# Wide tap products for half of the channels, loads from a second queue, and small re-cuts in a fused S4 convolution and MLP kernel

## The chip, the cores and the metric

The kernel runs on one core of one Trainium2 chip. The metric is the device time of one execution in microseconds (us); the median of several executions is compared. Five engines work side by side, each on its own list of instructions in a fixed order, and wait for each other by semaphores: PE (TensorE, matrix products into PSUM), DVE (VectorE), ACT (ScalarE), POOL (GpSimd), and SP (SyncE), which here only issues DMAs. A core has 16 DMA engines, shared by all queues.

## The reference, cut to what matters

Sequence length L = 2048, width D = 512, N = 128 modes for each channel, MLP width F = 1376, batch 1, all inputs bf16.

```python
# S4 mixer
dt = exp(log_dt)[:, None];  A = A_re + 1j*A_im
P = exp((dt*A)[:, :, None] * arange(L))               # 512 x 128 x 2048, complex
K = einsum("dn,dnl,dn->dl", C, P, dt*B).real          # one filter of 2048 taps for each channel
y = irfft(rfft(pad(u)) * rfft(pad(K)))[:L] + u*Dskip  # causal convolution by FFT of length 4096
# block
h  = x + S4(layernorm(x))
h2 = h + (gelu(layernorm(h) @ w1 + b1) @ w2 + b2)
```

The cost is in K: for each channel 2048 taps out of 128 complex modes, and in the two convolution transforms, which the kernel does as products.

## The kernel before, in words

**Taps.** A tap index l is the sum of a coarse and a fine part. For each channel d the kernel holds two small tables over the 128 modes (the modes lie on the partitions): EB/IB with NB = 33 coarse entries (real and imaginary part) and EA/IA with NA = 20 fine entries. The taps of a channel are then one product of 20 x 128 by 128 x 33, real and imaginary part summed in PSUM. The 512 channels are four chunks of 128 (CW); `kgen(c)` (from L1009) does one chunk. Its products have 20-column weights and 33 moving columns, and four channels stand at four column positions of the array, 32 rows apart: 256 products for a chunk (L1024 the real part, L1025 the imaginary one). The results are copied from PSUM to the tile `Kg` in two copies of 726 and 330 elements a partition.

**The tables.** Magnitudes come from exponentials on ACT: `bexps` (L738, 32 exponentials) for B and `aexps` (L948 to L953) for A, where PE adds up the exponents in PSUM with weights WA, a scaled identity for each step between entries; these scaled identities are made on ACT (L695) or DVE (L697) early. Phases come from `chain` (L959): PE adds integer phases step by step (L976 to L985), ACT takes the sine (L991), and DVE multiplies the table by sine and cosine (L1000 to L1002). There are four chains in this order: chunks 0 and 1, B and A, and chunks 2 and 3, B and A. GpSimd prepares the weights of the chains, among them the field words (L641 on).

**Convolution.** The signal (x after layer norm, `unorm`, L884) is transformed in `austage` (L897), written to DRAM (AU_d, one for each half of the sequence), read back in another layout (X0, XB; `xspec` L904), and finished by products (`fstage`, L923). The taps take the same way: `kspec` (L1061), the DRAM tensors AK_d, and `fstage`. `inverse` (L1085) multiplies the two spectra on DVE (L1101), transforms on PE (L1111), and a transposing DMA (`turn`, L1117) brings the result to ZT0 and ZT1, one tile for each chunk.

**Tails and MLP.** The rows are worked off in two halves b of two sub-blocks sb, each of four tiles j of 128 rows. `tail(b, sb)` (L1172) adds the residual x by a product with the identity (L1184), the convolution by products with DD (L1189), copies the sum from PSUM to `hs` and takes its statistics (L1194), normalises (L1208, L1210) and transposes. `mlp(b, sb)` (L1227) does 44 products (L1239), 11 gelus (L1241) and 44 products (L1256) of 512 columns, and adds h on DVE (L1258), which also frees PSUM, into one of three output tiles `ots`, from which two DMAs write 64 rows each.

**What sets the order.** Nothing of this is issued where it stands in the code. `S.add(engines, cost, function, reads, writes)` gathers all operations with planned costs and a priority `S.pr`. `S.run(NSL)` then lists them by a simulation of its own with four PSUM slots of 128 x 1024 f32 (`Ps()` takes one); `RANK`, a table of a place for each (priority, engine), breaks ties. `evac` (L530) lets the plan choose ACT (L533) or DVE (L535) for a copy out of PSUM. The instructions are emitted in the planned order, and each engine keeps it on the chip. Nearly all DMAs stand in the order of SP's list (`dma`, L543; L545).

The waits of the list that matter: a slot's next use waits for the copies out of it; `hs`, w1 and w2, and XB lie in memory that the tables held, so their loads wait for the products on these tables.

Of the kernel before, what the change touches and what calls it, by code (L numbers as in the profile page):

```python
# [145 lines left out]

class VS(V):
# [15 lines left out]
    "0S": 55, "0A": 268, "0.01A": 132, "0.02S": 110, "0.03A": 277, "0.04S": 66, "0.05S": 164, "0.1S": 223, "0.1A": 283, "0P": 86, "0.05P": 38,  # L163
    "0.1D": 241, "0.7D": 13, "0.75P": 173, "0.6P": 275, "0.72P": 230, "0.3D": 46, "0.1P": 244, "0.2P": 146, "0.05A": 95, "0.06A": 157, "0.07A": 106,
    "0.08A": 239, "0.09A": 193, "0.5D": 297, "0.5P": 290, "0.2A": 73, "0.2D": 2, "1.01A": 43, "1.015A": 131, "1.02A": 145, "1.025A": 229, "1.03A": 143,
    "1.035A": 342, "1.04A": 285, "1.045A": 121, "1.05A": 195, "1.055A": 316, "1.06A": 228, "1.065A": 181, "1.07A": 57, "1.075A": 11, "1.08A": 163,
    "1.085A": 84, "1.09A": 180, "1.095A": 25, "1.1A": 93, "1.105A": 155, "1.11A": 220, "1.115A": 29, "1.12A": 274, "1.125A": 255, "1.13A": 261,
    "1.135A": 133, "1.14A": 31, "1.145A": 170, "1.15A": 122, "1.155A": 337, "1.16A": 348, "1.165A": 62, "0.4A": 22, "0.4P": 254, "0.401A": 306,
    "0.4D": 12, "0.41D": 5, "0.42D": 71, "0.6A": 167, "0.6D": 212, "0.5S": 343, "0.55D": 78, "0.55S": 339, "1.5D": 90, "1.3P": 221, "1.55D": 309,
    "1.4P": 209, "1.5P": 51, "1.2D": 75, "1.201D": 79, "1.202D": 67, "1.203D": 35, "8D": 72, "8S": 213, "0.95P": 208, "0.95A": 17, "1.05P": 328,  # L170
    "1.15P": 253, "1.25P": 60, "1.25A": 191, "1.35P": 4, "1.35A": 105, "1.45P": 111, "1.45A": 246, "1.55P": 289, "1.55A": 325, "1.65P": 178,
    "1.65A": 299, "1.75P": 34, "1.75A": 242, "1.85P": 63, "1.85A": 45, "8A": 7, "1.3A": 102, "1.3D": 295, "1.7P": 219, "1.71P": 0, "1.9A": 58,
    "2.05P": 202, "1.8P": 42, "1.81P": 113, "2.11P": 26, "2P": 184, "2A": 324, "2D": 161, "2.1P": 112, "2.1A": 226, "2.1D": 207, "2.2P": 314,
    "2.2A": 280, "2.2D": 169, "2.3P": 340, "2.3A": 205, "2.3D": 83, "2.5P": 80, "2.5A": 187, "2.5D": 264, "2.6P": 320, "2.6A": 256, "2.6D": 152,
    "2.7P": 130, "2.7A": 298, "2.7D": 189, "2.8P": 96, "2.8A": 134, "2.8D": 101, "2.9P": 270, "2.9A": 1, "2.9D": 50, "2.94A": 27, "3.2D": 88,
    "4.1D": 117, "2.98A": 352, "2.96A": 326, "2.963A": 338, "2.966A": 162, "2.95A": 336, "4.5P": 350, "1.72P": 159, "3.4D": 284, "3.401D": 293,
    "3.402D": 115, "3.403D": 190, "3.5P": 149, "3.5A": 85, "3.5S": 251, "3.501P": 247, "3.501A": 312, "3.501S": 243, "4P": 302, "4A": 303, "4D": 234,
    "4.1P": 235, "4.1A": 345, "4.2P": 287, "4.2A": 135, "4.2D": 192, "4.3P": 39, "4.3A": 291, "4.3D": 174, "4.5A": 233, "4.5D": 301, "4.6P": 3,
    "4.6A": 91, "4.6D": 19, "4.7P": 292, "4.7A": 236, "4.7D": 154, "4.8P": 273, "4.8A": 259, "4.8D": 142, "4.9P": 310, "4.9A": 18, "4.9D": 151,
    "4.1S": 37, "4.101P": 271, "4.101A": 238, "4.101S": 116, "4.2S": 281, "4.201P": 222, "4.201A": 171, "4.202P": 41, "4.202A": 214, "4.203P": 6,  # L180
    "4.203A": 69, "5.1P": 36, "5.1A": 118, "5.11P": 108, "5.11A": 262, "5.11D": 89, "9.1P": 294, "9.1A": 266, "9.11P": 232, "9.11A": 198, "9.11D": 48,
    "9.2P": 147, "9.2A": 346, "9.21P": 218, "9.21A": 260, "10.2P": 224, "10.2A": 330, "10.21P": 124, "10.21A": 176, "10.2S": 20, "10.25S": 201,
    "10.25P": 166, "10.25A": 127, "10.251P": 240, "10.251A": 32, "10.252P": 99, "10.252A": 129, "10.253P": 168, "10.253A": 267, "10.3D": 64,
    "10.3P": 341, "10.3A": 329, "10.3S": 40, "10.4D": 47, "10.4P": 44, "10.4A": 182, "10.4S": 33, "13.1P": 318, "13.1A": 203, "13.11P": 179,
    "13.11A": 351, "13.11D": 103, "17.1P": 331, "17.1A": 197, "17.11P": 327, "17.11A": 120, "17.11D": 70, "17.2P": 165, "17.2A": 56, "17.21P": 237,
    "17.21A": 24, "17.2S": 49, "17.25S": 126, "17.25P": 141, "17.25A": 288, "17.251P": 104, "17.251A": 353, "18.2P": 278, "18.2A": 252, "18.21P": 300,
# [17 lines left out]
class Clock:  # L204
# [12 lines left out]
    def work(self, t, c, a):  # L217
        self.idle(t)
        while c > 1e-9:
            k = 1.0 if self.warm else 2.0  # L220
            d = min(c * k, self.end - t)
            t += d
            c -= d / k
            self.act += a * d / k
            if self.end - t < 1e-9:
                self.turn()
        return t


class Sched:  # L230
    def __init__(self):
        self.ops = []
        self.wr, self.rd = {}, {}
        self.pr = 0.0
# [174 lines left out]
def kernel(ctx, tc, A_u, A_A_re, A_A_im, A_B_re, A_B_im, A_C_re, A_C_im, A_log_dt, A_Dskip,  # L409
# [40 lines left out]
    def at(lo, dt, *shape):  # L450
        return V(ar, lo, dt, shape)
# [934 lines left out]
```

## Time and profile before

| what | us |
|---|---|
| median of 3 runs | 286.64 |
| the three runs | 286.47, 286.64, 288.91 |
| the profiled execution | 284.77 |
| its span | 283.0 |
| mean granted clock of PE | 0.957 |
| first exponential of `bexps` | 8.77 |
| end of the exponentials | 38.4 |
| first product of the first chain | 47.1 |
| end of the fourth chain | 102.2 |
| taps of chunks 2 and 3 | 103.8 to 126.4 |
| first product of the MLP | 189.1 |
| last output sum | 278.46 |

The span is what the profiler shows of the program; the execution's time has 1.8 us more around it. "Busy" of an engine counts its instructions' time without waits. An entry such as `L1101 DVE ar<-ar 128x1024 x48 | 30.0, 685` is a group: line, engine, operation, output and input, count, busy time in us and the mean of one in ns. Nearly all SBUF data lies in one large tile called `ar`. The chain of work that ended last follows back, from the last instruction, what released each step; "issue" in it is time in which an engine waited for nothing that the profile shows, "SPq" time in which SP's queue issued.

### The profile page before, as it was taken

How to read it: one execution, taken by the hardware profiler on the slowest of the kernel's cores; microseconds unless marked ns; L12 is line 12 of the kernel's file. 1: busy time of each engine (PE TensorE's matmuls, PEld its weight loads, DVE VectorE, ACT ScalarE, POOL GpSimd, SP SyncE). 2: the span in 40 equal slices, each digit the busy share in tenths (PEclk: the TensorE clock that was granted, in tenths of full speed). 3: DMA queues.
4: the chain of work that ended last, by engine and by line, in shares of the span. 5: the costliest groups of instructions: out<-in, count | busy, mean ns of one | idle time of the engine just before them, and what ended most of it. 6: DMA issues, size and time to landing. Idle time of an engine off the chain costs nothing.

```text
span 283.0 us, 7899 instructions
## 1 busy us (share of the span) xinstructions
PE 227.0 (80%) x3316; PEld 122.8 (43%) x3316; DVE 177.2 (63%) x380; ACT 176.5 (62%) x241; POOL 40.9 (14%) x213
## 2 busy tenths in 40 slices
PE   6407949679999897299978767879999989979973
PEld 2202413324577756243666653544343434434431
DVE  4999899999989770039979973876378320021020
ACT  5999999999959884046876733378326704603600
POOL 9991001006980000000000000000000000000000
PEclk9999986999999999869999995799999999999999
DMA  7950013879300008995279999951215310011011
GB/s 148 316 113 0 1 46 94 219 222 302 90 3 5 5 5 287 345 384 157 80 193 232 242 197 223 184 116 38 57 41 102 74 37 22 19 37 37 1 39 37
DMA packets 47878, 33.62 MB, mean 119 GB/s; under 512 B 29441, under 2 KB 43746, under 8 KB 47842
## 3 DMA queue, kind: packets, MB, share of 16 engines
q1 hardware_dynamic: 46642, 32.72, 45.6%
q8 instruction: 26, 0.43, 0.6%
q10 hardware_dynamic: 1200, 0.39, 0.6%
q14 instruction: 10, 0.08, 0.1%
HBM read 16.32 MB, written 10.49 MB: 95 GB/s over the span
## 4 chain that ended last, share of the span: by engine, by line
PE 46%; ACT 17%; DVE 15%; DMA 11%; issue 7%; SPq 2%; POOL 1%; DVEq 0%; ACTq 0%; POOLq 0%
PE ps L1239 14%; PE ps L1256 13%; DMA ar<-ar 6%; ACT ar L738 6%; ACT ar L533 4%; DVE ar L535 4%; PE ps L1024 3%; DMA ar<-AK_d 3%; PE ps L1025 3%; PE ps L923 3%; PE ps L1189 3%; DVE ar L1101 2%; ACT ar L991 2%; PE ps L985 2%; DVE ar L1258 2%
## 5 line engine op out<-in xcount | busy, mean ns | idle before, releaser
L533 ACT CAST ar<-ps 128x1024 bf16<-128x1024 f32 (+3 forms) x77 | 66.4, 907 | 54.6 <-PE ps L1025 15.2
L1241 ACT ACTIVATE ar<-ps,ar 128x512 bf16<-128x512 f32 (+1 forms) x44 | 29.9, 686 | 30.1 <-PE ps L1239 29.3
L1256 PE MATMUL ps<-ar 128*128 128x512 bf16 (+1 forms) x176 | 40.3, 379 | 5.0 <-DVE ar L1258 5.0
L1258 DVE TENSOR_TENSOR ar<-ps,ar 128x512 bf16<-128x512 f32 x16 | 11.0, 689 | 48.8 <-PE ps L1256 43.5
L535 DVE CAST ar<-ps 128x1024 bf16<-128x1024 f32 (+2 forms) x27 | 31.0, 1169 | 16.2 <-PE ps L923 13.0
L1239 PE MATMUL ps<-ar 128*128 128x512 bf16 (+1 forms) x176 | 39.1, 379 | 0.0
L991 ACT ACTIVATE ar<-ps 128x1024 bf16<-128x1024 int16 x36 | 35.2, 1066 | 2.3 <-issue 1.1
L1101 DVE TENSOR_TENSOR ar<-ar 128x1024 bf16<-128x1024 bf16 x48 | 30.0, 685 | 4.6 <-PE ps L1111 4.2
L1111 PE MATMUL ps<-ar 64*128 64x128 bf16 x768 | 26.9, 225 | 5.4 <-DVE ar L1101 4.5
L1256 PEld LDWEIGHTS <-ar 128*128 128x128 bf16 (+1 forms) x176 | 16.9, 98 | 27.4 <-issue 8.0
L1111 PEld LDWEIGHTS <-ar 64*128 64x128 bf16 x768 | 23.3, 99 | 10.1 <-DVE ar L1101 8.0
L581 POOL TENSOR_SCALAR ar<-ar 128x128 bf16<-128x128 bf16 (+5 forms) x40 | 24.8, 643 | 18.2 <-ACT ar L602 18.2
L1024 PE MATMUL ps<-ar 128*20 128x33 bf16 x512 | 19.9, 249 | 8.5 <-issue 7.9
L1239 PEld LDWEIGHTS <-ar 128*128 128x128 bf16 (+1 forms) x176 | 17.4, 100 | 20.6 <-issue 0.6
L985 PE MATMUL ps<-ar 128*32 128x256 f16 x560 | 21.4, 275 | 2.0 <-ACT ar L991 1.1
L1024 PEld LDWEIGHTS <-ar 128*20 128x20 bf16 x512 | 17.8, 124 | 10.7 <-issue 10.0
L923 PE MATMUL ps<-ar 128*64 128x512 bf16 (+1 forms) x160 | 19.2, 367 | 3.1 <-DMA ar<-AK_d 2.1
L1025 PE MATMUL ps<-ar 128*20 128x33 bf16 x512 | 19.9, 248 | 0.0
L1194 DVE BATCH_NORM_STATS2 ar<-ps 128x6 f32<-128x512 f32 x16 | 10.7, 691 | 13.5 <-ACT ar L533 7.9
L1001 DVE TENSOR_TENSOR ar<-ar 128x1024 bf16<-128x1024 bf16 x26 | 18.0, 711 | 1.7 <-ACT ar L991 1.6
L985 PEld LDWEIGHTS <-ar 128*32 128x32 f16 x560 | 13.8, 97 | 10.8 <-issue 9.8
L1002 DVE TENSOR_TENSOR ar<-ar 128x1024 bf16<-128x1024 bf16 x26 | 17.4, 697 | 1.6 <-ACT ar L991 1.5
(86 smaller groups left out, 265.0 us busy)
## 6 DMA issues: line engine op xcount, KB each, us to landing
AU_d<-ar SPq DMA_DIRECT2D x16, 256.0 KB, 4.6
ar<-AU_d SPq DMA_DIRECT2D x8, 512.0 KB, 5.2
ar<-AK_d SPq DMA_DIRECT2D x8, 512.0 KB, 7.8
ar<-in_A_u_dram SPq DMA_DIRECT2D x16, 128.0 KB, 3.8
ar<-in_A_u_dram SPq DMA_DIRECT2D x4, 512.0 KB, 5.7
AK_d<-ar SPq DMA_DIRECT2D x2, 1024.0 KB, 4.7
AK_d<-ar SPq DMA_DIRECT2D x4, 512.0 KB, 3.8
out_dram<-ar SPq DMA_DIRECT2D x32, 64.0 KB, 2.0
```

The lines of the kernel that those rows point to most:

```text
L533: act.copy(out_fn(), in_fn())
L535: dve.tensor_copy(out_fn(), in_fn())
L923: pe.matmul(pst(p)[64 * h:64 * h + 64, w * (k + r):w * (k + r) + w], lhsT=T.ap()[:, f, r, :], rhs=v.ap()[:, f, :], start=True, stop=True, ...
L985: pe.matmul(pst(p)[32 * g:32 * g + 32, 256 * j:256 * j + 256], lhsT=W2[DELTAS.index(d)].ap(), rhs=S2[g].ap()[:, ch0:ch0 + 256], start=Fals ...
L991: add("ACT", c_act(1024), lambda e, p=p, sc=sc, cs=cs: act.activation(sc[cs].ap().rearrange("p a b -> p (a b)"), pst(p, i16).rearrange("p ...
L1024: pe.matmul(o, lhsT=Ar.ap()[:, :, d], rhs=Br.ap()[:, :, d], start=True, stop=False, tile_position=(0, 32 * g))
L1025: pe.matmul(o, lhsT=Ai.ap()[:, :, d], rhs=Bi.ap()[:, :, d], start=False, stop=True, tile_position=(0, 32 * g))
L1101: dve.tensor_tensor(o, a, b_[:, :, ::-1, :] if sw else b_, ALU.mult)
L1111: pe.matmul(pst(p)[:, 512 * h + 128 * k:512 * h + 128 * k + 128], lhsT=q.ap()[rows, 2 * k + r, :], rhs=TP[w].ap()[rows, f0 // 2 + k, :], s ...
L1239: pe.matmul(pst(p)[:fs, 512 * z:512 * z + 512], lhsT=w1s[dc].ap()[:, fc * P:fc * P + fs], rhs=ybuf.ap().rearrange("p (t c) k -> p c t k", ...
L1241: add("ACT", c_act(512, 1), lambda e, p=p, z=z, fc=fc, fs=fs: act.activation(hT.ap()[:fs, fc, :], pst(p)[:fs, 512 * z:512 * z + 512], ACT. ...
L1256: pe.matmul(pst(p)[:, 512 * z:512 * z + 512], lhsT=hT.ap()[:fs, fc, 128 * t:128 * t + 128], rhs=w2s[fc].ap()[:fs], start=(fc == 0), stop=( ...
```

## The change

- *Taps of chunks 2 and 3.* `kgen4` replaces `kgen` there. EA2 and IA2 hold these chunks' A tables channel by channel, 20 entries padded to 32, so that four channels are 128 weights. One product takes them with 132 moving columns (four channels of 33). Of the 4 x 4 blocks of the result only the four on the diagonal are wanted: each is copied by itself, 32 partitions of up to 198 elements. The pads are cleared by GpSimd. 64 products a chunk replace 256, and 24 copies replace 2.
- *Tables.* `aexps` goes by halves of 256 channels, four entries an exponential; the second half writes the new layout. WA has 20 scaled identities (steps of 12 entries instead of 6), made by GpSimd. The last chain's sines and products on DVE work in the new layout (runs of 4 elements). Raw inputs are transposed by products with a permuted identity, which puts the channels in an order that suits the new taps.
- *Loads.* x, w1, w2, b2 and the second half's signal spectrum (XB) are issued by GpSimd's queue, in fewer and larger DMAs; SP keeps the inputs of the start, AU_d of the first half, AK_d, the transposes and the output. The plan knows both queues, and a transpose waits in the plan for what is in transfer.
- *Layer norm.* The inverse square root takes two iterations with other constants, not three: four small operations fewer.
- *Tails.* All but the first take the residual on DVE, which adds `hs` to PSUM and takes the statistics from SBUF; the product with the identity and the copy go.
- *Output.* Eight tiles `ots` instead of three.
- *Plan.* All entries of `RANK` are new, so the order moves everywhere. On SP the reads of AK_d for chunks 2 and 3 now stand after three of the four writes. In the last product of each MLP sub-block the four tiles' products alternate otherwise.

```diff
+    def pad(v, k):
+        POOL(3.3, lambda: gp.memset(v.ap().rearrange("p c d a -> p (c d) a")[:, :, NA:32], 0.0), w=[v], pr=k)
...
-    LD = [LA[a] - (LA[a - 6] if a >= 6 else 0) for a in range(NA)]
+    LD = [LA[a] - (LA[a - 12] if a >= 12 else 0) for a in range(NA)]
...
+        PTS(WA[n], identb, float(v), pr=0.8 + 0.01 * (n // 4))
...
-        for _ in range(3):
+        for m, k in ((-1.0, c1), (-0.5 * c0 ** 3, 1.5 * c0)):
...
+    def kgen4(c, pr):
+        Ar, Br, Ai, Bi = EA2[c - 2], EB[c], IA2[c - 2], IB[c]
+        kg = Kg[c // 2]
+        for j0 in range(0, 32, 6):
...
+            p = Ps()
+            n = min(6, 32 - j0)
+            h = (n + 1) // 2
+            for b in range(2):
+                def fn(e, p=p, j0=j0, b=b, h=h):
+                    for jj in range(h):
+                        i = j0 + h * b + jj
+                        o = pst(p)[:, 512 * b + 132 * jj:512 * b + 132 * jj + 132].rearrange("p (k g) -> p k g", g=4)
+                        pe.matmul(o, lhsT=Ar[4 * i:4 * i + 4].ap().rearrange("p d a -> p (d a)"), rhs=Br.ap()[:, :, 4 * i:4 * i + 4], start=True, stop=False)
+                        pe.matmul(o, lhsT=Ai[4 * i:4 * i + 4].ap().rearrange("p d a -> p (d a)"), rhs=Bi.ap()[:, :, 4 * i:4 * i + 4], start=False, stop=True)
...
+            for g in range(4):
+                rows = slice(32 * g, 32 * g + 32)
...
+                evac(ofn, ifn, 2 * h * NB + 80, [p], [kg.part(32 * g, 32 * g + 32)])
...
-    ots = [at(BA0 + 51200 + 1024 * n, bf16, 512) for n in range(3)]
+    ots = [at(sc0 + 8192 + 1024 * n, bf16, 512) for n in range(8)]
...
-            dma("SP", lambda c=c: w1s[c].ap(), lambda c=c: B_w1[128 * c:128 * c + 128, :], 352256, [], [w1s[c]], soft=[("KFR", 0, (0, 1), fh) for fh in range(4)], pr=pr + 0.1 * c)
+            dma("POOL", lambda c=c: w1s[c].ap(), lambda c=c: B_w1[128 * c:128 * c + 128, :], 352256, [], [w1s[c]], pr=pr + 0.1 * c, k=0.7)
...
-                    pe.matmul(o, lhsT=identb.ap(), rhs=hs[8 * b + j].ap(), start=True, stop=False)
+                    if first:
+                        pe.matmul(o, lhsT=identb.ap(), rhs=hs[8 * b + j].ap(), start=True, stop=False)
...
+                if not first:
+                    add("DVE", c_dve(512, 1, True), lambda e, src=src, hh=hh: dve.tensor_tensor(hh.ap(), src(), hh.ap(), ALU.add), r=[p, hh], w=[hh], hv=0, soft=[y2s[0]] if sb else [])
...
-            kgen(c, 5.1 + 4 * c)
+            (kgen if q == 0 else kgen4)(c, 5.1 + 4 * c)
...
-    xspec(1, XB, 50)
+    xspec(1, Two(XB), 18.8, q_="POOL")
```

## The prediction, made before the changed kernel had run

> **What bounds the kernel now.** I read the page's totals, then busy time by stage, then the chain of work that ended last, then the groups and waits of the lines that it names. The cuts of the stages are events: 38.4 the last exponential, 102.2 the end of the index chains, 189.1 the first MLP product. T below is 102.2, and "T+20" is 20 us after the end of the index chains in either kernel.
>
> ```profile
> PE 227.0 (80%) x3316; PEld 122.8 (43%) x3316; DVE 177.2 (63%) x380; ACT 176.5 (62%) x241; POOL 40.9 (14%) x213
> ```
>
> TensorE at 80% looks like the bound. The busy time by stage says otherwise (start:end, length, busy of PE, PEld, DVE, ACT, POOL with instructions, granted clock, DMA share, GB/s):
>
> ```profile
> 0.00:38.40 38.40, 20.68 (x84) 8.78 (x84) 32.88 (x83) 35.14 (x69) 21.66 (x179) 1.00 0.43 109
> 38.40:102.20 63.80, 54.80 (x1214) 31.24 (x1218) 59.27 (x111) 57.92 (x66) 18.73 (x33) 0.95 0.38 108
> 102.20:189.10 86.90, 67.25 (x1634) 46.46 (x1622) 55.72 (x94) 46.58 (x52) 0.52 (x1) 0.90 0.83 210
> 189.10:283.00 93.90, 84.30 (x394) 36.31 (x392) 29.38 (x93) 36.87 (x56) 0.00 (x0) 1.00 0.21 45
> 110.00:120.00 10.00, 2.61 (x145) 2.26 (x137) 0.18 (x1) 0.43 (x1) 0.00 (x0) 0.93 1.00 328
> ```
>
> Up to T, ACT and DVE set the pace (DVE idles 4.5 us of 63.8). From T to 189.1 no engine is full and the DMA share is 0.83: that stage is waits. In the last stage PE is 90% busy. The fifth row is a hole: for 10 us no engine works and the DMA engines are full. The chain names it "issue", and shows two transfers behind it:
>
> ```profile
> 110.18 1.91 issue
> 114.45 5.48 issue
> ...
> 137.93 5.61 ACT ar L533 x6
> 143.56 0.37 SPq L545
> 144.03 6.28 DMA ar<-AK_d
> ...
> 161.60 12.35 DMA ar<-ar x2
> ```
>
> The hole lies in the taps of chunks 2 and 3 (L1024, L1025), 256 tiny products a chunk. I read it as TensorE's own instructions arriving late behind 6 loads and reads of data. The Trainium skill agrees (Runtime: NRT & Kernel Launch, Instruction fetch mechanics): a sequencer fetches its code by its own DMA queue in blocks of 256 instructions. The 12.35 us are two of the three transposes issued at 161.6 between loads of x and w2. The last stage shows the third kind of wait, six of these, 0.84 us each:
>
> ```profile
> PE ps L1256 <- DVE ar L1258: 5.0, 6, 0.8
> ```
>
> **Up to T.** Scaling the WA products leaves ACT (16, of which 7 take 1.5 us from 4.53, 8 take 1.69 from 7.18) and DVE (3). The second 8 stand before the first exponential at 8.77 while its operand is ready at 7.58, so ACT starts some 1 us earlier. GpSimd takes 20 in their place: its 128x128 products in bf16 take 0.57 alone (25 in 14.25 us from 66.16) and 1.1 beside DVE (4 in 4.50 us from 79.08), so 11.4 to 22 us; I take 0.72, the shorter of the two of this very form (128x128 f16 from bf16, L676 and L677, 0.83 and 0.72): 14.4. Two pads of 3072 elements are new (a 928-element memset takes 0.87: 2.9 each). The exponentials of A are 10 instead of 10 of 1024, PE's products for them 104 instead of 52, of half the width. DVE saves 4 small operations of 0.19 in its statistics (0.8) and 3 scalings (0.4). The second A chain has 10 products on DVE with 8-byte runs: 0.69 (like the reversed form of L1001, which costs what the straight one does) up to 1.22 (DVE's 1024-element copy from PSUM), so 0 to +5 us; I take the nearest row, 0.69. DVE gets one AU copy more (1.2). GpSimd's field words move behind its 20 products, and DVE and PE wait for them: I estimate these words at 35 us where the chain starts at 47, so nothing, up to +5 if each product costs 1.1. Sum: **+1 us, from −4 to +5**.
>
> **From T to the first MLP product (87.0 before).**
> - Taps. PE gets 64 products of 128 weights a chunk in place of 256 of 20. A 128-weight product of 128 columns takes 0.073 (L1218, 16 in 1.17), so 64 of 132 columns 4.8 us, against 4.3 now (8 in 0.135): nothing. The instruction stream of those chunks falls to a quarter, and the hole (1.91+5.48 = 7.4) should go. But the copies out of PSUM rise from 4 to 48 for both chunks: 40 of 198 elements and 8 of 66, on 32 partitions each. From 330 in 0.448 and 726 in 0.773 on ACT (0.82 ns an element over 0.18) a 198 takes 0.34; DVE (726 in 0.902, 1024 in 1.22) 0.37. The order of instructions gives 27 to ACT and 21 to DVE: 9 and 7 us against 3.3 and 0.9. So ACT +5.8, DVE +6, both in a stretch (103.8 to 126.4) where ACT works 7.5 us and DVE 3.75. They hide there. If 32-partition copies with 16-byte steps in PSUM cost twice as much, ACT has 18 us, still inside 22.6: cover is gone only past 3 times.
> - What is late next. PE runs in order, and the first products on K's spectrum (KF0) stand in PE's order before the last tap round. KF0 arrives at T+18.5 now; after, its write ends later since ACT has more ahead of it (T+11.7 instead of T+7.2), and its reads no longer share the engines with AU and w1 reads: T+21. So the taps end at T+26.5 instead of T+24.3: **+2.2**. The hole goes and its gain is not cashed there.
> - AK_d of chunks 2 and 3. Now the 4 writes stand in SP's order ahead of the reads (SP: 131.47, 12.46 us for 4), and the reads start 17.6 us after the taps. In the new order the 2 reads stand after 3 writes. By the same copies (6 on ACT 5.61 now) the third write is issued 12.5 us after the taps: T+39 instead of T+41.9: **−5.1** relative to the taps.
> - Its read took 6.28 while a transpose and w2 loads ran. A 512 KB AU read lands in 5.2: **−1.2**.
> - Transposes. SP's queue loses 5.3 MB of loads (x 2, w1 1.4, w2 1.4, the last XB). One transpose alone takes 2.2 to 3 us (2.10 at 187.80, 3.00 at 180.61), so two 5 to 6 in place of 12.35: −6.5. The inverse (L1101, products of 0.69 on DVE) is then next: DVE has 60 us of work in 78.5 (56 in 87 now), and I take 3 back for it: **−3.6**.
> - The tail of the first sub-block stays, but its statistics lose 4 operations of 0.19: **−0.8**.
> - Sum: 2.2 − 5.1 − 1.2 − 3.6 − 0.8 = **−8.5**. Bounds: −14 (hole and transposes in full: 7.4 + 6.5) to −3 (only the write order, less the taps' delay).
>
> **MLP stage (93.9 before).** The 8 identity products of the later tails in it go, at 0.31 (198.64 to 198.95): 2.5. The DVE sums that replace them (12 of 0.69) lie on an engine busy 29 of 94 us. With the new order of products 2 of the 6 waits of 0.84 remain: 3.4. Eight output tiles in place of 3 give nothing, as no wait on a tile shows. **−6, from −4 to −7**, as nothing else can replace so full a PE.
>
> **Sum.** +1 − 8.5 − 6 = −13.5 on the profiled execution's 284.77: 271.3. The median of the runs shown, 286.64, stands 1.87 above it, so **273** as a median.
>
> One rule of the Trainium skill speaks against the change: SBUF — State Buffer, "DVE blocks DMA" says that a DMA issued from GpSimd has its descriptors written by GpSimd through a port pair that VectorE can lock. No GpSimd load of data is in this trace; the nearest row is its own products beside VectorE, 0.57 to 1.1. By that ratio the 16 us of loads (below) become 32 and end at T+58; w1 is needed at T+78.5 and XB a little before it, so the sum would stay.
>
> **Rivals.**
> - *Collision* (0.17). GpSimd's loads do not wait in SP's order, so all 5.3 MB start together once the taps release their memory (T+26) and take 16 us at the 328 GB/s of the hole: to T+42, across the AK_d write and read. For: the 12.35 us above come from such a meeting. Against: AK_d now has reads of its own at T+39, when most has landed. If the AK_d round trip takes what the transposes gained, 6.5 goes back: **279.5**.
> - *More is released* (0.14). The taps end with the hole gone in full, and T comes early: a further 6 to 10, **265**. For: 7.4 us of stall. Against: KF0 in PE's order.
> - *GpSimd bounds the start* (0.12, slower). Field words and pads stand behind 20 products in GpSimd's order, and DVE, then PE's first chain, wait for them in their own orders. Chain start is 47.1; with products at 1.1 (22 us instead of 14.4) and pads and iotas doubled the words come at 50 to 62. It loses 1 us for each past 47.1 and passes before's time once they are later than about 60.6 (13.5 us); then about **289**. For: GpSimd 21.7 of 38.4 us busy now, and 20 us more. Against: 1.1 was seen only beside DVE's two-input operations, few before 38.
> - *The wide taps do not do what they say* (0.07). Copies of 32 partitions cost 3 times my 0.34 (1.0, as for 1024 elements): 48 give 24 us on each of two engines, 17 past what hides: the slot wait puts about 10 on the taps, **283**.
>
> **How the numbers follow.** Forecast 0.50 with a spread of 268 to 277. The range takes in the collision, the copies and the faster case: **263 to 284**; outside lie the slow start (0.12) and the far end of the fast case, 0.05. About 1% (2.9 us; the three runs shown span 2.4) can be told from no change: faster by over 1% means below 283.8. Slower: 0.09 of the slow start and 0.02 of the copies, 0.11; same: 0.03 of each, 0.06; faster **0.83**.
>
> **What would show it.** Right: no "issue" of over 1 us between T+5 and T+25; taps as 64 products a chunk with 198-element copies of 0.3 to 0.4; reads of AK_d for chunk 2 at T+39; no transpose over 4 us; L1256's successors waiting for DVE twice. Wrong: AK_d reads over 8 us (collision), first chain later than 49 (GpSimd), PE waiting for ACT's small copies, DVE's strided products over 0.9. The forecast fails outright if the copies cost as much as whole ones, or if instructions still arrive late because GpSimd's loads now fill the same DMA engines while PE is fetching the inverse's products.

## The result, and the profile after

The changed kernel takes 352.4 us (median; 350.8 to 353.3) against 286.8 of the kernel before: ratio 1.2295, 95% interval 1.2212 to 1.2378. I had forecast 273, with a range up to 284. The profiled execution has a span of 349.0 us. (Single executions of a kernel can take over 1.5% longer than its fastest; ratios here compare the others.) The line of totals:

```profile
PE 247.3 (71%) x2960; PEld 146.2 (42%) x2972; DVE 215.5 (62%) x387; ACT 237.2 (68%) x239; POOL 75.4 (22%) x257
```

ACT is busy 60.7 us longer than before with two instructions less, DVE 38.3 longer with seven more, PE 20 longer with 356 fewer. So it is not waits in the first place: the same instructions take longer. By stage of the changed kernel (start:end, length, busy us of PE, PEld, DVE, ACT, POOL with counts, granted clock, DMA share, GB/s); the cuts are the first exponential of the new kind, the last one, the end of the index chains, and the first MLP product:

```profile
0.00:34.70 34.70, 18.05 (x98) 10.56 (x98) 27.67 (x57) 27.27 (x46) 30.98 (x200) 1.00 0.36 96
34.70:58.30 23.60, 6.75 (x40) 4.26 (x38) 10.37 (x37) 23.57 (x7) 0.20 (x1) 0.73 0.04 11
58.30:151.30 93.00, 66.03 (x1193) 43.78 (x1200) 70.12 (x93) 81.25 (x62) 32.01 (x35) 0.87 0.21 53
151.30:260.10 108.80, 73.87 (x1259) 51.39 (x1253) 75.45 (x113) 73.56 (x80) 12.15 (x21) 0.80 0.75 192
260.10:349.00 88.90, 82.63 (x380) 36.25 (x383) 31.92 (x89) 31.57 (x48) 0.00 (x0) 0.98 0.22 47
```

The second row is 23.6 us in which ACT runs seven instructions and the others mostly wait for it. The chains end at 151.3 instead of 102.2 (+49); from there to the MLP it is 108.8 instead of 87.0 (+22); only the last stage is shorter, 88.9 instead of 93.9 (−5). The groups with shapes kept apart (count | busy us, mean ns | idle before, releasers) name the instructions, first in the changed kernel:

```profile
L992 ACT ACTIVATE ar<-ps 128x1024 bf16<-128x1024 f32 x5 | 22.7, 4831 | 0.7 <-PE ps L985 0.7
L989 ACT ACTIVATE ar<-ps 128x1024 bf16<-128x1024 f32 x5 | 4.9, 1014 | 0.1
L561 ACT CAST ar<-ps 32x198 bf16<-32x198 f32 x22 | 22.8, 1035 | 10.8 <-DVE ar L563 10.2 <-PE ps L1102 0.4
L563 DVE CAST ar<-ps 32x198 bf16<-32x198 f32 x18 | 18.7, 1038 | 16.1 <-ACT ar L561 15.9
L1072 PE MATMUL ps<-ar 128*20 128x33 bf16 x256 | 21.9, 402 | 0.9 <-DVE ar L563 0.9
```

The rows of the kernel before to hold beside them, a sine, a chain product and a product of kgen:

```profile
L991 ACT ACTIVATE ar<-ps 128x1024 bf16<-128x1024 int16 x36 | 35.2, 1066 | 2.3 <-issue 1.1 <-DVE ar L1001 0.7 <-PE ps L985 0.5
L1002 DVE TENSOR_TENSOR ar<-ar 128x1024 bf16<-128x1024 bf16 x26 | 17.4, 697 | 1.6 <-ACT ar L991 1.5
L1024 PE MATMUL ps<-ar 128*20 128x33 bf16 x512 | 19.9, 249 | 8.5 <-issue 7.9 <-DVE ar L1002 0.3 <-DVE ar L535 0.3
```

L989 and L992 are the same exponential of the same 1024 elements, for the first and second half of the channels; the second writes element by element with 64 bytes between neighbours, and takes 4.8 times as long. The small copies take 1.04 us on either engine, where I had 0.34 and 0.37, and each engine waits for the other's. And kgen of chunks 0 and 1, whose products I had not touched in the sum, takes 0.40 us a product (0.249 before). Beside it others suffer. From the timeline of DVE and ACT (start, length), around the first burst of kgen, which begins at 91.72, and in a stretch without it:

```profile
90.67 0.68 DVE L1049 TENSOR_TENSOR ar<-ar 128x1024 bf16<-128x1024 bf16 x1
91.46 2.29 DVE L1050 TENSOR_TENSOR ar<-ar 128x1024 bf16<-128x1024 bf16 x1
...
107.96 0.69 DVE L1050 TENSOR_TENSOR ar<-ar 128x1024 bf16<-128x1024 bf16 x1
```

```profile
89.12 14.17 ACT L1030 ACTIVATE ar<-ps 128x1024 bf16<-128x1024 int16 x8 [0.33 <-PE ps L1024]
...
135.39 2.46 ACT L1030 ACTIVATE ar<-ps 128x1024 bf16<-128x1024 int16 x1
```

A chain product on DVE is 0.68 before the burst, 2.29 in it and 0.69 in a pause. Eight sines beside kgen take 14.17 us (1.77 each, 1.03 alone). The last row is a sine of the fourth chain, when kgen is over: it writes every 8 bytes and takes 2.46 by itself.

So there were four suspects, all in how data lies in SBUF: the exponentials' writes, the sines' writes, the copies' writes, and kgen's reads.

### The profile page after: what moved, and what is told of

It reads as the page before. It is cut to its first block, busy times and chain, and to the rows that moved or that the text cites. A ratio compares the mean times of both kernels' runs of the same rounds, so it can differ in the third digit from the quotient of the medians.

```text
span 349.0 us, 7267 instructions
## 1 busy us (share of the span) xinstructions
PE 247.3 (71%) x2960; PEld 146.2 (42%) x2972; DVE 215.5 (62%) x387; ACT 237.2 (68%) x239; POOL 75.4 (22%) x257
## 4 chain that ended last, share of the span: by engine, by line
PE 41%; ACT 24%; DVE 21%; issue 8%; DMA 3%; SPq 1%; DVEq 0%; ACTq 0%
PE ps L1318 11%; PE ps L1335 10%; ACT ar L561 10%; DVE ar L563 7%; ACT ar L992 6%; PE ps L1186 6%; ACT ar L1030 6%; DVE ar L1049 4%; DVE ar L1050 4%; PE ps L952 2%; PE ps L1136 2%; PE ps L1264 2%; PE ps L985 2%; DVE ar L618 2%; DMA ar<-in_A_A_re_dram 1%
## 5 line engine op out<-in xcount | busy, mean ns | idle before, releaser
L561 ACT CAST ar<-ps 128x1024 bf16<-128x1024 f32 (+4 forms) x92 | 85.4, 970 | 31.9 <-DVE ar L563 10.2
L1030 ACT ACTIVATE ar<-ps 128x1024 bf16<-128x1024 int16 x36 | 62.4, 1919 | 11.6 <-DVE ar L1050 5.1
L563 DVE CAST ar<-ps 128x1024 bf16<-128x1024 f32 (+4 forms) x46 | 49.4, 1081 | 29.2 <-ACT ar L561 16.5
L609 POOL TENSOR_SCALAR ar<-ar 128x128 bf16<-128x128 bf16 (+6 forms) x60 | 42.9, 737 | 21.8 <-ACT ar L630 20.4
L1024 PE MATMUL ps<-ar 128*32 128x256 f16 x560 | 24.0, 299 | 17.1 <-ACT ar L1030 16.4
L1176 DVE TENSOR_TENSOR ar<-ar 128x1024 bf16<-128x1024 bf16 x48 | 30.0, 686 | 5.4 <-PE ps L1186 5.0
L952 PE MATMUL ps<-ar 128*64 128x512 bf16 (+1 forms) x160 | 22.1, 410 | 12.5 <-DVE ar L563 4.8
L992 ACT ACTIVATE ar<-ps 128x1024 bf16<-128x1024 f32 x5 | 22.7, 4831 | 0.7 <-PE ps L985 0.7
L926 PE MATMUL ps<-ar 128*128 128x512 bf16 x25 | 8.8, 420 | 19.5 <-DVE ar L607 16.6
L1072 PE MATMUL ps<-ar 128*20 128x33 bf16 x256 | 21.9, 402 | 0.9 <-DVE ar L563 0.9
L1073 PE MATMUL ps<-ar 128*20 128x33 bf16 x256 | 22.0, 402 | 0.0
L1049 DVE TENSOR_TENSOR ar<-ar 128x1024 bf16<-128x1024 bf16 x21 | 21.6, 1054 | 0.1
L1050 DVE TENSOR_TENSOR ar<-ar 128x1024 bf16<-128x1024 bf16 x21 | 20.9, 1017 | 0.5 <-ACT ar L1030 0.2
```

Of the source, the lines that this page charges most:

```text
L561: act.copy(out_fn(), in_fn())
L563: dve.tensor_copy(out_fn(), in_fn())
L609: en.tensor_scalar(a, b, f(s1), f(s2), op0, op1)
L992: add("ACT", c_act(1024), lambda e, p=p, n=n: act.activation(dmaj(EA2, 4 * n).rearrange("p x a -> p a x"), pst(p).rearrange("p (a x) -> p ...
L1024: pe.matmul(pst(p)[32 * g:32 * g + 32, 256 * j:256 * j + 256], lhsT=W2[DELTAS.index(d)].ap(), rhs=S2[g].ap()[:, ch0:ch0 + 256], start=Fals ...
L1030: add("ACT", c_act(1024), lambda e, p=p, sc=sc, cs=cs: act.activation(sc[cs].ap().rearrange("p a b -> p (a b)").rearrange("p (x a) -> p a ...
```

## The experiments

### Each suspect undone by itself, then all four

The first four kernels ran once each, so a difference of 1 or 2 us between them says nothing.

The exponentials. The destination stays, only the order in which it is written turns, so that four entries (8 bytes) of a channel come one after another:

```diff
-act.activation(dmaj(EA2, 4 * n).rearrange("p x a -> p a x"), pst(p).rearrange("p (a x) -> p a x", a=4), ACT.Exp)
+act.activation(dmaj(EA2, 4 * n), pst(p).rearrange("p (a x) -> p x a", a=4), ACT.Exp)
```

> The changed kernel with one loop turned: the five exponentials of the second half of the A table (4.83 us each in the changed kernel, 1.01 for the five of the first half) write channel by channel, four entries of 8 bytes together, instead of entry by entry with 64 bytes between neighbours. Theory (a write whose neighbours lie 64 bytes apart costs 4.6 ns an element on ACT): they take 1.0 to 1.4 us, ACT reaches the chains 17 to 19 us earlier, the total falls from 352 to 333 to 336. Rival 1 (the size of the destination's pitch costs, whatever the order): still over 4 us, no change of the total. Rival 2 (GpSimd's late field words bound the start): the exponentials get short, but the first chain starts no earlier and the total stays within 3 us.

Measured: 338.1 us, 14.3 less; the five exponentials take 1.02 us each, and the chains end at 136.4 instead of 151.3. The total fell by less than the 19 us that ACT saves, since DVE had 10.4 us of work of its own in those 23.6, and lies above the 333 to 336 that the theory gave. Its mechanism holds: the pitch of the destination stayed at 64 bytes and cost nothing once neighbours are written together.

The sines of the fourth chain, turned in the same way (`sc` written without gaps, PSUM read in large steps):

```diff
-sc[cs].ap()[...].rearrange("p (x a) -> p a x", a=4)  <-  pst(p, i16).rearrange("p (a x two) -> p a x two", ...)
+sc[cs].ap()[...].rearrange("p (x a) -> p x a", a=4)  <-  pst(p, i16).rearrange("p (a x two) -> p x a two", ...)
```

> The changed kernel with one loop turned: the ten sines of the last chain write contiguously and read PSUM with steps of 1024 bytes, instead of writing every 8 bytes. Theory: these ten take about 1.05 us instead of 2.44 (and less than 5.8 beside kgen), the last chain ends 10 to 16 us earlier, the total falls to 336 to 344. Rival (reading PSUM with large steps costs as much): they stay over 2 us.

Measured: 338.3 us, 14.1 less; all 36 sines together went from 62.4 us to 45.0, and the chains end at 139.3.

The small copies:

```diff
-return kg.ap()[rows, :, c & 1, j0:j0 + 2 * h].rearrange("p k (b i) -> p b i k", b=2)
+return kg.ap()[rows, :, c & 1, j0:j0 + 2 * h].rearrange("p k (b i) -> p k b i", b=2)
-... .rearrange("p b (i k g) -> p b i k g", i=h, g=4)[:, :, :, :, g]
+... .rearrange("p b (i k g) -> p k b i g", i=h, g=4)[:, :, :, :, g]
```

> The changed kernel with the loops of the 48 small copies turned, so that six channels (12 bytes) are written together instead of single elements 128 bytes apart; the PSUM side is read with steps of 528 bytes instead of 16. Theory (scattered writes cost): a 198-element copy takes 0.34 to 0.5 us instead of 1.035, the taps of chunks 2 and 3 end 20 to 28 us earlier, the total falls to 325 to 334. Rival 1 (32-partition copies or steps in PSUM cost, not the writes): still about 1 us, or more; no change. Rival 2 (the taps wait for the spectrum of the first taps, and the loads on GpSimd's queue hold the rest): the copies get short, but the total falls by less than 10.

Measured: 338.6 us, 13.8 less. A copy of 198 elements takes 0.316 on ACT and 0.361 on DVE, almost my 0.34 and 0.37. The taps of chunks 2 and 3 take 19.7 us instead of 45.9, but the total fell by half of that, less than the theory's 325 to 334 asked for. The rival, that what follows is held by something else, was half right. In this kernel PE waits 11.0 us for reads of AK_d before its next products, a wait that the changed kernel doesn't have; the write of AK_d ahead of them takes 24.9 us here, beside the loads:

```profile
L952 PE MATMUL ps<-ar 128*64 128x512 bf16 x96 | 16.2, 456 | 14.3 <-DMA ar<-AK_d 11.0 <-ACT ar L1030 1.4 <-DVE ar L563 0.9
```

The reads of kgen: chunks 0 and 1 keep the plain identity for their transposes (and `dtb` in plain order), and with it the channel order of the kernel before:

```diff
-                                d = 4 * (i0 + i) + g
+                                d = 32 * g + i0 + i
...
-rhs=identp.ap()
+rhs=(identb if d < 2 else identp).ap()
```

> The changed kernel with the channel order of chunks 0 and 1 as in the kernel before: the four products that run side by side in kgen read columns 64 bytes apart instead of neighbours of 2 bytes. Theory (four readers in one line of SBUF slow each other and whoever else goes to SBUF): kgen's products go from 0.40 us to about 0.25, VectorE's chain products beside them from 2.3 to 4.1 us to 0.7, the sines of the second B chain from 1.77 to about 1.0; the chains end 12 to 22 us earlier and the total falls to 330 to 340. Rival (the new places of the tables in memory, or GpSimd's work, slow the chains): kgen at 0.40 and the chain products over 2 us as before, the total within 4 us.

Measured: 334.8 us, 17.6 less; the chains end at 132.4. DVE's chain products (L1052 here) are back at 0.704 from 1.054, and kgen's products at 0.249. The granted clock does not explain this: its mean was 0.867 in this kernel and 0.878 in the changed one.

All four:

> All four turns together: exponentials, sines of the last chain (8-byte steps, 2.44 us each, now contiguous), small copies, and kgen's channel order. Theory (the 66 us lost are the price of scattered writes and reads alone, 17 to 19 for the exponentials, about 14 for the sines, 12 to 22 for kgen's neighbours, 18 to 27 for the copies): the time falls to 270 to 285, near the predicted 273, with no ACT instruction over 1.4 us. Rival 1 (GpSimd's queue and its loads, or the longer start of GpSimd, also cost): it stops at 290 to 305, with the extra time between the last chain and the MLP, or before the first chain. Rival 2 (the order of the plan does not fit the real durations): above 300.

Measured: 290.2 us (289.8 to 290.8), ratio to before 1.0108 (1.0048 to 1.0167). The single steps sum to 59.8 us, all four together give 62.2, so they hardly overlap and account for 62 of the 65.6 us lost. But 290 is not 273: of what was expected for this run, the rival with the extra time between the chains and the MLP came in, and not the theory's 270 to 285. The stages of this kernel, in the same columns as above:

```profile
0.00:38.40 38.40, 21.11 (x126) 13.17 (x127) 31.23 (x71) 29.42 (x49) 31.12 (x201) 1.00 0.32 87
38.40:105.70 67.30, 51.54 (x1205) 31.35 (x1210) 61.31 (x116) 59.59 (x66) 29.75 (x35) 0.95 0.29 76
105.70:200.10 94.40, 65.35 (x1257) 45.67 (x1253) 61.96 (x112) 56.43 (x80) 12.15 (x21) 0.87 0.91 222
200.10:289.00 88.90, 82.63 (x380) 36.31 (x383) 32.66 (x90) 31.66 (x47) 0.00 (x0) 0.98 0.22 46
```

The chains end at 105.7 (forecast 103.2), the last stage lasts 88.9 (forecast 87.9), and the middle 94.4 where I had 78.5. Its DMA share is 0.91, and its chain of work that ended last has one step that stands out:

```profile
116.51 23.91 DMA AK_d<-ar
140.47 7.20 DMA ar<-AK_d
```

The first taps' spectrum is written in two transfers of 1 MB. The second, shown here, needs 24 us. In the kernel before it was issued at 109.01 and the reads behind it started at 114.55, so it had 5.5. GpSimd's queue issues its loads from 112.8 on. What the two queues moved between 122 and 138 us (packets, MB, share of the 16 engines' time), q0 being GpSimd's loads and q1 this write:

```profile
q0 software_dynamic: 978, 3.64, 80.7%
q1 hardware_dynamic: 972, 0.99, 21.7%
```

The packets are equal in number, but a packet of the write holds 1 KB and one of the loads 3.7 KB on average. So the write got about a fifth of what was moved. It reads as if the engines took packets of the two queues by turns; no run here varies the size of a packet to test that.

### The price of a write, by itself

Copies of 512 bf16 elements a partition, behind the last operation of the kernel before:

> The kernel before with copies appended behind its last operation, three times each, of 512 bf16 elements a partition: on ACT and DVE from PSUM, written without gaps and with 4, 8, 16, 32, 64 and 128 bytes between neighbours, in runs of 2 and of 4 elements at 64 bytes, read from PSUM with steps of 512 bytes, and with SBUF operands read without gaps and at 64 bytes. It is for the durations of these, not the total. Theory (a write pays for each 16 or 32 bytes of SBUF that it touches anew): without gaps 0.53 on ACT and 0.6 on DVE; 4 bytes about the same; 8 bytes 1.2 to 1.4; 64 bytes 2.3 to 2.5; runs of 4 at 64 bytes 0.55 to 0.8; reads at any step as without gaps. Rival (only the count of elements and the step of 64 bytes or more counts): 8 and 16 bytes cost as without gaps. Rival (reads pay as writes do): the two operands at 64 bytes take over 2 us.

Measured, one row for each kind of copy (min/median/max ns of three): ACT from PSUM, written without gaps, then with 4, 8, 16 and 64 bytes from one element to the next, then in runs of two elements at 64 bytes; after these, ACT from SBUF without gaps and read at 64 bytes:

```profile
L1361 ACT CAST ar<-ps x3: 586/586/587, 276.1 to 308.1; 128x512 bf16<-128x512 f32 x3
L1362 ACT CAST ar<-ps x3: 727/727/732, 276.7 to 308.7; 128x512 bf16<-128x512 f32 x3
L1363 ACT CAST ar<-ps x3: 1289/1290/1295, 277.5 to 309.4; 128x512 bf16<-128x512 f32 x3
L1364 ACT CAST ar<-ps x3: 2419/2419/2437, 278.8 to 310.8; 128x512 bf16<-128x512 f32 x3
...
L1366 ACT CAST ar<-ps x3: 2377/2377/2377, 283.7 to 315.5; 128x512 bf16<-128x512 f32 x3
...
L1368 ACT CAST ar<-ps x3: 587/587/587, 288.6 to 320.4; 128x512 bf16<-128x512 f32 x3
...
L1371 ACT COPY ar<-ar x3: 617/618/618, 290.4 to 322.3; 128x512 bf16<-128x512 bf16 x3
L1372 ACT COPY ar<-ar x3: 1044/1045/1045, 291.1 to 322.9; 128x512 bf16<-128x512 bf16 x3
```

DVE gives the same rows to 2 ns from 8 bytes on (1.290, 2.420, 2.292, 2.377, 2.432), with 0.692 without gaps. Less a fixed 0.17 us (my estimate from the rows at 8 and 16 bytes), a lone element costs 4.4 ns from 16 bytes apart on, half of that at 8 bytes and a quarter at 4: about 4.4 ns for each 16 bytes of SBUF in which single 2-byte elements are written. Two elements written together, 4 bytes, cost nothing, at a pitch of 64 bytes too. Large steps in PSUM on the reading side cost nothing (0.586); SBUF reads at 64 bytes cost 1.7 times on ACT (above) and 2.4 times for a two-input product on DVE (1.014 against 0.426), so my expectation that reads are free at any step was off. The Trainium skill says (SBUF — State Buffer, Specifications) that lines of 16 bytes need two hits each for full bandwidth. The 16 bytes agree with these rows; the two hits do not: two lone elements a line cost 1.29, and a single pair of elements costs 0.587.

### The reads of four column groups, by themselves

In the kernel before, one line of kgen, for all chunks:

```diff
-                                d = 32 * g + i0 + i
+                                d = 4 * (i0 + i) + g
```

> The kernel before with one edit: kgen of all four chunks takes channel 4(i0+i)+g in place of 32g+i0+i, so that the four products side by side read neighbours of 2 bytes instead of columns 64 bytes apart (the taps get a wrong channel order; the work is the same, instruction by instruction). Theory (four readers in one line of SBUF): kgen's products go from 0.25 to about 0.40 us, VectorE's chain products beside them from 0.69 to 2 to 4 us, the chains end 10 to 20 us later and the total is 298 to 312. Rival (only the changed kernel's memory layout makes this slow): kgen stays at 0.25, the total within 3 us of 286.6.

Measured: 311.6 us (the faster of two runs; the other took 317.7), 25 more than before, from strides alone. The products and the chain products on DVE beside them:

```profile
L1024 PE MATMUL ps<-ar 128*20 128x33 bf16 x512 | 42.6, 402 | 0.7 <-DVE ar L1002 0.3 <-DVE ar L535 0.3
L1002 DVE TENSOR_TENSOR ar<-ar 128x1024 bf16<-128x1024 bf16 x26 | 32.8, 1288 | 0.4 <-ACT ar L991 0.3
```

One of those 26 took 7.77 us. Then with 16 and 32 bytes between the four columns, other channel orders of the same work:

> The kernel before with one edit in kgen: the four products that run side by side read columns 16 bytes apart (channel 8g + i mod 8 + 32 (i div 8)), in place of 64 bytes; the taps get another channel order, the work is the same. With 2 bytes between them a product took 0.40 us in place of 0.25 and the total was 315. If readers hinder each other within 16 bytes, as lone writes of 2 bytes cost by 16-byte pieces: 0.25 us and 284 to 290. If the piece is larger (32 or 64 bytes): 0.30 to 0.40 us, chain products on VectorE over 1 us, total 295 to 316.

> The same with 32 bytes between the four columns (channel 16g + i mod 16 + 64 (i div 16)). If the piece in which readers hinder each other is 16 or 32 bytes: 0.25 us a product and 284 to 290. If it is 64: 0.30 to 0.40 and 295 to 316.

Measured: 287.0 and 288.0 us, one run each (before on the same chip 286.1). At 16 bytes:

```profile
L1024 PE MATMUL ps<-ar 128*20 128x33 bf16 x512 | 20.0, 249 | 8.0 <-issue 7.1 <-DVE ar L1002 0.3 <-DVE ar L535 0.3
```

So products that run side by side hinder each other, and the instructions of DVE and ACT beside them, when their columns lie 2 bytes apart; at 16 bytes they don't. Distances between 2 and 16 bytes were not measured. The Trainium skill (SBUF — State Buffer, Who interferes with whom) has PE and ACT wait for nobody and only the port pair of DVE and GpSimd contended; the rows of 402 ns for PE and 1.77 us for a sine beside it say otherwise here.

### The loads on the second queue

First the queue itself: the four turns, and all of GpSimd's loads on SP's queue (`q = "SP"` in `dma`), which lets the plan place them.

> The four turns of the loops, with all loads on SP's queue as in the kernel before (the plan puts them into SP's order, so their places change). It tells what the second queue itself is worth. If the loads' collision with AK_d is a matter of the queue, this is 272 to 282 and the AK_d write for chunks 0 and 1 takes under 10 us; if loads in SP's order delay the AK_d reads and transposes as they did before, 283 to 292.

Measured: 298.9 us, slower than with two queues (290.2) and outside both ranges. SP's order now holds the AK_d reads behind loads, which stand in it from 115.8 to 127, and the first MLP product comes at 210.3. The second write of the first spectrum takes 11.9 us on the one queue too, so the meeting with loads is not a matter of the second queue alone.

Then the loads stay on GpSimd's queue and wait, behind an instruction that reads what must have landed:

```diff
+POOL: tensor_scalar(gt, KF0[:, ::4, 0:1], 1.0, 1.0, mult, mult)   # reads KF0 after its four DMAs
 POOL: 17 loads of XB, x, w1, w2, b2
```

> The four turns of the loops, and one more edit: GpSimd's 17 load instructions stand behind a small GpSimd instruction that reads the first taps' spectrum (KF0) after its four reads from DRAM, so that no load of x, w1, w2 or XB is issued before they have landed. Nothing else moves. With the four turns alone the write of AK_d for chunks 0 and 1 takes 23.9 us (4.7 in the kernel before) while these loads run, and KF0 arrives 42 us after the last chain. Theory (the loads on the second queue hold the AK_d write up): the write takes 5 to 8 us, the first MLP product comes 75 to 84 us after the last chain instead of 94, the total is 271 to 280. Rival 1 (the write is slow for itself, by its layout or by transposes and code): still over 15 us, the total within 4 us of 290. Rival 2 (the loads now meet the write and read of AK_d for chunks 2 and 3): that pair takes over 25 us, and the total is 281 to 290.

> The four turns of the loops, and two gates on GpSimd's queue in place of one: the four XB reads stand behind an instruction that reads KF0 (the spectrum of the first taps, after its reads from DRAM), and the loads of x, w1 and w2 behind one that reads the first part of the spectrum of chunks 2 and 3. With one gate for all, the AK_d write of chunks 0 and 1 fell from 23.9 us to 5.6, and the write of chunks 2 and 3 then took 17.6 beside the loads. Theory (whatever of these loads meets an AK_d write is paid on the path): AK_d's first write 5 to 8 us, the next 6 to 12 (XB's 2 MB still meet it), the first MLP product at 180 to 188 us instead of 200, the total 270 to 279. Rival (the loads, now later, meet the transposes and the MLP waits for x or w1): the first MLP product after 192, the total 281 to 292.

In these two the new tile `gt` moves all later tiles by 8 bytes, which changes what the kernel computes, so I rest the argument on the times of their transfers and not on their totals. With one gate the slow write lands in 5.6 us instead of 23.9: the loads are its cause. But the total is 295.5 us: the AK_d write of chunks 2 and 3 now takes 17.6. With two gates PE stands 9.8 us before the products on XB, and a transpose that meets the loads takes 26 us: 302.0. With `gt` in dead memory, and XB free:

> The four turns of the loops; the four XB reads are issued as early as GpSimd's queue allows, and the loads of x, w1 and w2 stand behind an instruction that reads KF0 (written into memory that nothing uses any more, so that no tile moves). Theory (each load that meets an AK_d write is paid): XB's 2 MB delay the first AK_d write from 5.6 to 10 to 14 us, the 3.3 MB of the rest delay the second by as much, the first MLP product comes at 188 to 196, the total is 278 to 287. Rival (moving the loads only moves the collision, and the sum stays): 288 to 296.

> The four turns of the loops; each load of GpSimd's queue stands behind an instruction that reads what the load before it brought, so that one is in transfer at a time and not up to eight. Theory (the AK_d write is slow because several loads share the DMA engines with it): the first AK_d write falls from 23.9 to 8 to 14 us, KF0 comes some 10 us earlier, the first MLP product at 184 to 194, the total 274 to 285. Rival (what is in transfer does not matter, the bytes do): the write stays over 18 us and the total at 287 to 295.

Measured: 289.5 us for the first (ratio 1.0046, 1.001 to 1.0083), the same as without a gate; 302.8 (1.037 to 1.0569) with one load at a time. The chain of the first:

```profile
115.99 10.94 DMA AK_d<-ar
128.33 8.83 DMA ar<-AK_d
...
144.53 17.57 DMA ar<-AK_d
```

Thirteen us are gained at the write (10.9 for 23.9), and a later read of AK_d takes 17.6, where the longest on the chain was 7.2 without the gate. Paced, the write is quick (6.9 us, its reads start at 124.5), but PE waits in its order for XB, which now comes in pieces until 143.8. So how many loads are in transfer sets the time of the write (23.9 beside 17 loads, 10.9 beside four, 5.6 with none), but not the total: the DMA share of this stretch was 0.91 with the four turns, and in each order tried some other transfer that PE waits for became late. Whether an order without such a meeting exists I did not find, and leave open.

### Parts of the MLP stage in the kernel before

Residual on DVE in later tails and eight output tiles, with the old RANK:

> The kernel before with two parts of the change alone: the residual on VectorE in all tails but the first, and eight output tiles (in the place that the changed kernel gives them); the plan keeps the RANK of before. It isolates the term of the MLP stage: the stage lasted 93.9 us before and 88.9 both in the changed kernel and with the four turns, where I had forecast a gain of 6. Theory (8 identity products of 0.31 and part of the six waits of 0.84): 281 to 284.5, ratio 0.98 to 0.993, and the first MLP product within 2 us of 189.1. Rival (these gains need the new plan's order of products; with the old one VectorE's sums come late for the second tails): 285 to 290, with PE waiting for L1276's successors or for VectorE.

Measured: 294.4 us, ratio 1.019 (1.0143 to 1.0237). The rival was right in kind and too small: 294.4 is beyond its 285 to 290 too. The plan sets DVE's sums for a later tail behind others, and the third sub-block's products wait for their transpose:

```profile
PE ps L1244 <- DMA ar<-ar: 10.2, 1, 10.2
```

Eight tiles alone:

> The kernel before with eight output tiles alone. The plan, which no longer has to wait for a free tile, then alternates the products of the four tiles of a sub-block (11 of one, 4 of another, 11 of the first, the rest), as in the changed kernel; identity products and copies stay. Theory (four of the six waits of 0.84 for VectorE's sums go): PE's waits in the last products fall from 5.0 us to 1.7 to 2.5, the total by 2.5 to 3.4, ratio 0.988 to 0.992. Rival (as with the tails, a part of the change taken alone shifts the plan somewhere else and costs more than it gains): 286 to 292, with a new wait in the MLP stage.

Measured: 285.2 us, ratio 0.9948 (0.9905 to 0.9992), the one kernel here that is faster than before, by half a per cent where I had expected about one. Of the six waits of 5.0 us three are left, of 2.5, as expected, and the stage from 189.1 lasts 91.7 instead of 93.9:

```profile
PE ps L1256 <- DVE ar L1258: 2.5, 3, 0.9
```

## Why the prediction was wrong

- **The step that failed** is the pricing of instructions whose operands are laid out anew by their count and element count alone. "The exponentials of A are 10 instead of 10 of 1024" and the sines of the second A chain stood in my sum at nothing; they cost 14 us each, measured singly. I bounded DVE's 8-byte runs (0.69 to 1.22, right: 0.69 to 0.70 where kgen was not running) and looked only at the reading side of the copies, "16-byte steps in PSUM", when it was the write.
- **What I left out altogether**: the permuted identity changes the channel order for chunks 0 and 1 too, and with it which columns kgen's four groups read at once. It stood in my own description of the change, without a price: 17.6 us.
- **The copies.** My rival "the wide taps do not do what they say" had the price right, 1.0 us a copy (1.035), and its reason wrong: not the 32 partitions. Its effect I put at 10 us by two engines in parallel. They were not parallel: the emitted copies of one round wait for each other across engines (16.5 and 10.2 us in the changed kernel; with the four turns, between 104 and 135 us, 3.8 and 3.5). Two readings beside it were off without bearing on the sum: DVE's copy rows give 0.34 and not 0.37 (0.361 was measured), and the copies of chunks 2 and 3 in the kernel before took ACT 2.4 us and DVE none, since DVE's one copy of 726 belongs to chunk 1. These are the waits in the changed kernel:

```profile
DVE ar L563 <- ACT ar L561: 16.5, 10, 3.0
...
ACT ar L561 <- DVE ar L563: 10.2, 7, 3.3
```

- **The hole** of the instruction feed is gone, as forecast: in the kernel with four turns no wait of PE for "issue" between 104 and 135 us is over 0.8, against 5.48 (16 and 32 bytes between kgen's columns, with the old taps, left it at 7.1 and 7.4 in all); and as forecast it is not cashed. That instructions arrive late, which the prediction argued, can be read in the trace of the kernel before: 16 KB blocks on the instruction queue (q8) end at 110.53, 118.43 and 124.62 us, and PE goes on 1.5 us after each, at 112.09, 119.93 and 126.12.
- **The middle stage**, without the four errors, is 94.4 where I had 78.5. This is my rival *Collision*, at 0.17. I put the loads at T+26 and across the second AK_d write; they are issued from T+7 (112.8), as soon as the first tap rounds release memory, and meet the first. The stage is 16 us longer than the sum, where the rival had 6.5. The write of 23.9 us in place of 5.5 puts the first taps' spectrum at T+42, where I had T+21. The loads of the second queue moved 7.0 MB and not 5.3, since all four reads of XB went there; at the 328 GB/s that I used they fill 21 us, not 16. How the 16 us divide beyond the write stays open: no run that moved the loads brought the total down.
- **The start.** T came at +3.5 in the kernel with four turns, inside −4 to +5. The scalings cost GpSimd 0.400 us each, not 0.72 (7.6 us, not 14.4), and the pads 2.66 (2.9). The slow-start rival has no part in the loss. One thing shows the port between the two engines, in the changed kernel:

```profile
7.34 2.66 POOL L1346 MEMSET ar<- 128x3072 bf16 x1
7.34 2.93 DVE L607 TENSOR_SCALAR ar<-ar 128x512 f16<-128x512 f32 x1
```

DVE's product, 0.41 us in the kernel before, ends just after the pad of GpSimd that began with it. The Trainium skill (SBUF — State Buffer, Who interferes with whom) describes such a lock for a DVE operation in a fast mode beside GpSimd, and this row agrees. For DMAs issued by GpSimd, the use that I had made of the page, these runs show no effect of DVE: the 512 KB reads on its queue land in 5.6 us in the changed kernel, 5.2 on SP's before. (With the four turns, where they meet the slow write, it is 9.9.)
- **The MLP stage**: −5.0 (88.9 against 93.9) for −6. It is right in mechanism: PE's waits for DVE's sums fell from 5.0 to 1.7 us. It needs the new plan's order: two of the five us come with eight tiles alone, which I had priced at nothing because no wait on a tile shows. The tiles act through the plan, which alternates products when it need not wait for a tile.

## What to carry to other kernels

For each operand that an edit lays out anew, write down what lies between two elements that are written one after the other: an innermost run of two bf16 elements was enough, and one alone cost about 4.4 ns for each 16 bytes touched: at 16 bytes 4.1 times a plain copy on ACT and 3.5 times on DVE. Turning the loop was free where the source is PSUM (0.586); where it is SBUF, a read at 64 bytes cost 1.7 times on ACT. Where several small products share the array, keep the columns that they read at one time at least 16 bytes apart (2 cost 25 us here, 16 nothing). And a second queue brought no second set of DMA engines: in a stretch whose share was already 0.83, the loads that were free of one queue's order made a write of small packets four times as long.

## What I had not expected of the hardware

A product on PE that reads badly slows the others more than itself: 0.25 to 0.40 us for PE, but for a product on DVE beside it 0.70 to 1.29 on average over the whole group, and 7.8 once. And the four losses add up almost exactly (59.8 singly, 62.2 together), since each sat on another piece of the path: the exponentials, sines and kgen's reads moved the end of the chains by 14.9, 12.0 and 18.9 us singly and by 45.6 together, and the copies lie in the taps behind it.
